# Moving the transposes of x from TensorE to VectorE's 32 by 32 blocks, with the scores on sixteen tiles, in a cross-attention and SwiGLU kernel on Trainium2

## The chip, the cores and the metric

One core of a Trainium2 chip. The time is the device time of one execution in microseconds (us).

## The reference

Eight batches of 512 tokens and 32 states, 8 heads of 64 columns, all fp32. Tokens read the states and states read the tokens through one product of scores; both results go through one gated feed-forward block.

```python
# x: (8, 8, 512, 64), state: (8, 8, 32, 64) = (B, H, S or Ns, D)
scores  = scale * x @ state^T ;   a  = softmax(scores)  ; xread = a  @ state
scores2 = scale * state @ x^T ;   a2 = softmax(scores2) ; sread = a2 @ x
tok = concat([xread, sread], axis=2)  -> (B*(512+32), 512)
xn  = tok / sqrt(mean(tok^2) + 1e-6) * rms_g          # w_gate, w_val: 512 x 1536, w_out: 1536 x 512
out = (silu(xn @ w_gate) * (xn @ w_val)) @ w_out
```

## The kernel before

Each batch is a period of some 87 us. A period holds the feed-forward of batch b (the "hidden half", six pairs of seven block products each, then the "projection") and, spread between its products, the attention of batch b+1. The order in which all engines get their instructions is a string of letters, one letter a step of one stream: `a` the read of the tokens, `s` the read of the states, `h`, `t`, `u` products, copies and sums of the hidden half, `p`, `c`, `k` those of the projection, `v`, `w`, `x` the products of the weights with the states.

The part that the change replaces: x is turned by sixteen full transposes on TensorE, ScalarE copies them out of the accumulator, and the scores are eight matmuls on tiles of 64 rows by 32 columns (a tile is a part of TensorE's array; the profile writes it `64*32`).

```python
def tokens_read(b):
    ...
    TE.transpose(out=tp, in_=packed, identity=ident)              # the states of b      L272
    VE.tensor_copy(stT, tp)
    xT = one.tile([P, 4, NC, P], F32, name="xT", tag="xT")
    for c in range(NC):                                            # NC = 4
        tp = aps.tile([P, 4, P], F32, name="at")
        for j in range(4):
            TE.transpose(out=tp[:, j, :], in_=xb[:, c, P * j:P * j + P], identity=ident)  # L282
        yield
        SE.copy(xT[:, :, c, :], tp)                                                       # L284
        yield "step"
    sp = [aps.tile([P, S], F32, name="at") for e in range(2)]
    for j in range(4):
        for e in range(2):
            TE.matmul(out=sp[e][Ns * j:Ns * j + Ns, :], lhsT=stT[D * e:D * e + D, j, :],  # L291
                      rhs=xT[D * e:D * e + D, j].rearrange("p c t -> p (c t)"),
                      start=True, stop=True)
    ...                      # 32 by 32 transposes on VectorE, softmax, transposes back

for b in range(1, B):        # the periods
    if b + 2 < B:
        load_state(b + 2)
        load_x(b + 2)        # 4 pieces of 256 KB, one queue
    ...
    for stream in PERIOD:    # the string: one letter, one step
        next(streams[stream])
```

Of the kernel before, what the change touches and what calls it, by code (L numbers as in the profile page):

```python
# [8 lines left out]
F32 = mybir.dt.float32  # L9
# [19 lines left out]
)  # L29

PERIOD = (
    "hthtvvhhtuxxhuhthuhththuuhtuuhhxxhhuvxutvhtthuuhuhthuuxhxhxuxtthuhuthhuthuxxhuta"
    "uahatuhtaxuuuhtauahuahhaahuttuhutauhhhtuuahuhuutauphuauupuauapacasapaaaapapaskaa"
    "aaksacccassppakckpaaackasaapakapaskaaaswpksksswsxxwxxpxcspcskx"
)

STATES = (
    "hyyyyhthyytthhhuuhtuhththhytuuhuuhthuhhtthyuhyyutyhhhuuuttyuhhutyyhhthuhyhuhuttu"
    "yhuhttyuhuhuuhuthhyuthythytuhuuhuhutuuhuuppcpkpcpukkcpkpkpc"
)  # L40


# [1 line left out]
def kernel(  # L44
# [7 lines left out]
    moe_rms_g: bass.AP,  # L52
    out: bass.AP,
):



# [38 lines left out]


    rows = {}
    x_sb = {}

    def load_state(b):

        rows[b] = two.tile([P, 2, D], F32, name="rows")
        for j in range(4):
            src = state[b, 2 * j:2 * j + 2].rearrange("e n d -> n e d")
            nc.sync.dma_start(out=rows[b][Ns * j:Ns * j + Ns], in_=src)

    def load_x(b, *queues):
        x_sb[b] = two.tile([P, NC, H * D], F32, name="x_b")
        for c in range(NC):  # L110
            (queues or (nc.sync,))[c % max(1, len(queues))].dma_start(
                out=x_sb[b][:, c].rearrange("p (h d) -> p h d", h=H),
                in_=x[b, :, P * c:P * c + P, :].rearrange("h p d -> p h d"))
# [150 lines left out]

    read = {}

    def tokens_read(b):
        xb, packed = x_sb[b], rows.pop(b)
        stT = two.tile([P, 4, Ns], F32, name="stT")
        stT_g[b] = two.tile([P, 4, Ns], F32, name="stT_g")  # L270
        tp = aps.tile([P, 4, Ns], F32, name="at")
        TE.transpose(out=tp.rearrange("p j n -> p (j n)"),  # L272
                     in_=packed.rearrange("p e d -> p (e d)"), identity=ident)
# [5 lines that stand above are left out]
        for c in range(NC):  # L279
# [15 lines that stand above are left out]


        sS = read[b] = two.tile([P, 2, NC, P], F32, name="sS")
        eS = one.tile([P, 2, S // Ns, Ns], F32, name="eS", tag="eS")
        m1 = two.tile([P, 2, S // Ns], F32, name="m1")
        z1 = two.tile([P, 2, S // Ns], F32, name="z1")  # L300
        for e in range(2):
            VE.transpose(out=eS[:, e].rearrange("p k n -> p (k n)"), in_=sp[e])
            yield
            SE.copy(sS[:, e].rearrange("p c t -> p (c t)"), sp[e])
            yield "step" if e else None

        def along(t, e):
            return t[:, e].unsqueeze(2).to_broadcast([P, S // Ns, Ns])

        for e in range(2):  # L310
            VE.reduce_max(out=m1[:, e], in_=eS[:, e], axis=AXX)
            yield
            VE.tensor_tensor(out=eS[:, e], in0=eS[:, e], in1=along(m1, e), op=ALU.subtract)
            yield
            SE.activation(out=eS[:, e], in_=eS[:, e], func=ACTF.Exp, scale=SCALE)
            yield "step"
        VE.tensor_tensor(out=stT_g[b], in0=stT, in1=rms_g.unsqueeze(2).to_broadcast([P, 4, Ns]),
                         op=ALU.mult)
        yield
        aT_s[b] = two.tile([P, 2, S], F32, name="aT_s")  # L320
        for e in range(2):
            VE.reduce_sum(out=z1[:, e], in_=eS[:, e], axis=AXX)
            yield
            VE.tensor_scalar(z1[:, e], z1[:, e], 1e-9, None, op0=ALU.add)
            VE.reciprocal(z1[:, e], z1[:, e])
            yield
            VE.tensor_tensor(out=eS[:, e], in0=eS[:, e], in1=along(z1, e), op=ALU.mult)
            yield
            VE.transpose(out=aT_s[b][:, e], in_=eS[:, e].rearrange("p k n -> p (k n)"))
            yield "step"  # L330


        reads = [(aps, vps)[j // 2].tile([P, S], F32, name=("at", "pv")[j // 2]) for j in range(4)]
        for j in range(4):
            for e in range(2):
                TE.matmul(out=reads[j][D * e:D * e + D, :],  # L336
                          lhsT=packed[Ns * j:Ns * j + Ns, e, :],
                          rhs=aT_s[b][Ns * j:Ns * j + Ns, e],
                          start=True, stop=True)
        yield  # L340
        sq = one.tile([P, 4, S], F32, name="sq", tag="xT")
        for i, j in enumerate((2, 3, 0, 1)):
            SE.activation(out=sq[:, i, :], in_=reads[j], func=ACTF.Square, scale=DM ** -0.5)
            yield "step" if i == 3 else None
        for i, j in ((0, 1), (2, 3), (0, 2)):
            VE.tensor_tensor(out=sq[:, i, :], in0=sq[:, i, :], in1=sq[:, j, :], op=ALU.add)
            yield
        sp = aps.tile([P, NC], F32, name="at")
        for c in range(NC):
            TE.matmul(out=sp[:, c:c + 1], lhsT=sq[:, 0, P * c:P * c + P], rhs=ones,  # L350
                      start=True, stop=True)
        yield
        ss = two.tile([P, NC], F32, name="ss")
        VE.tensor_scalar(ss, sp, 1e-6, None, op0=ALU.add)  # L354
        yield "step"
        ri = mean_root(ss, NC)
        yield
        rp = along_rows(ri, NC)
        yield
        VE.tensor_tensor(out=aT_s[b], in0=aT_s[b],  # L360
                         in1=rp.unsqueeze(1).to_broadcast([P, 2, S]), op=ALU.mult)
        yield "step"
# [160 lines left out]
    def weights_of(b):  # L523


        def blocks(mp):
            v, _ = v_sb[b, mp]
            return [[v[:, e, :, k, :]] for k in range(2) for e in range(2)]

        def sums(mp):  # L530
            _, vs = v_sb.pop((b, mp))
            return [[vs[:, i]] for i in range(3)]

        return blocks, sums
# [55 lines left out]
    def hidden_seven(n, weights, tokens, silu, after=lambda mp: None):  # L590
# [67 lines left out]
        def sums():  # L658
            for mp, q in enumerate(pairs):
                h = hb[:, 2 * mp:2 * mp + 2, 0:n]  # L660
                for to, ps in ((gates(q)[1], "z"), (gates(q)[0], "y"), (q["c"], "x")):
                    VE.tensor_tensor(out=to, in0=to, in1=q[ps][:, :, 0:half], op=ALU.add)  # L662
                    yield
                if not silu:
                    VE.scalar_tensor_tensor(out=h, in0=h, scalar=1.0, op0=ALU.add, op1=ALU.mult,  # L665
                                            in1=q["g"].rearrange("p m c t -> p m (c t)"))
                    yield
                for i, val in ((1, q["c"]), (0, q["x"][:, :, 0:half])):
                    part = h[:, :, half * i:half * i + half]
                    if silu:  # L670
                        VE.tensor_tensor(out=part, in0=part, in1=val, op=ALU.mult)
                    else:
                        VE.scalar_tensor_tensor(out=part, in0=part, scalar=0.5, in1=val,
                                                op0=ALU.mult, op1=ALU.mult)
                    yield
                if 2 * mp >= HM:
                    k = 2 * mp - HM
                    upper, lower = (hb[:, k:k + 2, half * i:half * i + half] for i in range(2))
                    VE.tensor_tensor(out=seven["s"][:, k:k + 2, 0:half], in0=lower,
                                     in1=h[:, :, half:n], op=ALU.add)  # L680
                    yield
                    VE.tensor_tensor(out=lower, in0=upper, in1=lower, op=ALU.subtract)
                    yield

        return products(), copies(), sums()
# [211 lines left out]
    for b in range(1, B):  # L897
        if b + 2 < B:
            load_state(b + 2)
            load_x(b + 2)  # L900
        h, t, u = hidden_seven(S, weights_of(b), lambda b=b: tokens_of(b), False)
        p, c, k = project_seven(S, store_tokens(b))
        own = [own_weights(b, mp) for mp in range(2, NM // 2)]
# [55 lines left out]
```

## Time and profile before

| | before |
|---|---|
| median of 4 runs (the rounds of the changed kernel) | 800.76 us (800.35 to 801.38) |
| span of the profiled run | 798.9 us |
| opening (to the first states' product of batch 1) | 133.65 us |
| one middle period | 86.90 us |
| from the last batch's states' product to the end | 148.11 us |

The three parts come from the starts of one kind of matmul that occurs once a batch (L397, the states' product with x): the distance between two of them is one period. In the same way I add up, for every kind of matmul, the distances from each record's start to the next start on TensorE. That sum is what the kind costs on a full TensorE, with its pipelining taken into account. The durations of single records are not: the profile's groups for one period (line, engine, operation, names, tile shape and operand, count, then busy us and mean ns of one) give 273 ns for a transpose of x, four of which hold TensorE for only 0.44 us.

```profile
L282 PE MATMUL at<-ident,x_b 128*128 128x128 f32 x16 | 2.4, 273 | 0.0
...
L291 PE MATMUL at<-xT,stT 64*32 64x512 f32 x16 | 1.1, 601 | 0.0
```

### The profile page before, as it was taken

The page shows a single profiled execution, that of the slowest core. Times are in us where ns is not written, and L with a number is a line of the kernel's source. Part 1 is how long each engine was busy: PE and PEld are TensorE (multiplying, and loading weights), DVE is VectorE, ACT ScalarE, POOL GpSimd, SP SyncE. Part 2 cuts the span into 40 slices and gives each one's busy share as a digit, 9 for nine tenths or more (in the row PEclk, how much of TensorE's full clock was granted, in tenths as well). Part 3 has the DMA queues.
Part 4 walks back from the last instruction along what each step waited for, and adds up shares of the span by engine and source line. Part 5 has one row for each costly group of instructions (what it writes and reads, how often), then busy time and mean ns, then how long its engine had stood idle before and what let it go on. Part 6 is the DMA issues. An engine that isn't in the chain of part 4 may idle for free.

```text
span 798.9 us, 12273 instructions
## 1 busy us (share of the span) xinstructions
PE 786.0 (98%) x4902; PEld 605.2 (76%) x4902; DVE 515.0 (64%) x786; ACT 347.0 (43%) x572; POOL 179.0 (22%) x216
## 2 busy tenths in 40 slices
PE   6999999999999999999999999999999999999998
PEld 5643444788778887888778877888788877888996
DVE  4999996688347842786358833785278635881461
ACT  5998864553245323543255314532354324510320
POOL 0000003530154004510433015500451044400000
PEclk9999999999999999999999999999999999999999
DMA  9987746700182007400461018200540024101311
GB/s 285 262 289 287 263 159 186 264 23 14 34 273 106 1 24 218 185 1 16 127 240 44 4 34 283 107 1 14 193 163 2 14 109 181 66 4 43 113 54 28
DMA packets 61593, 94.13 MB, mean 118 GB/s; under 512 B 38752, under 2 KB 46432, under 8 KB 54624
## 3 DMA queue, kind: packets, MB, share of 16 engines
q1 hardware_dynamic: 59360, 92.75, 34.2%
q10 hardware_dynamic: 2176, 0.59, 0.3%
q8 instruction: 39, 0.64, 0.3%
q14 instruction: 18, 0.15, 0.1%
HBM read 78.12 MB, written 15.20 MB: 117 GB/s over the span
## 4 chain that ended last, share of the span: by engine, by line
PE 93%; DVE 5%; issue 0%; DMA 0%; ACT 0%; SPq 0%
PE f L600 37%; PE f L754 35%; PE f L694 5%; PE pv L496 3%; PE at L454 3%; PE pv L454 3%; PE at L282 2%; PE at L291 1%; DVE ex L232 1%; PE at L397 1%; PE at L336 1%; DVE raw L228 1%; PE at L350 1%; PE at L385 1%; DVE w_m L237 1%
## 5 line engine op out<-in xcount | busy, mean ns | idle before, releaser
L754 PE MATMUL f<-wo,hb 128*128 128x256 f32 x540 | 124.2, 382 | 0.4 <-ACT ot L791 0.2
L662 DVE TENSOR_TENSOR g<-g,f 128x512 f32<-128x512 f32 (+1 forms) x96 | 62.8, 654 | 90.1 <-PE f L600 86.6
L600 PE MATMUL f<-aT_s,v 128*128 128x256 f32 x504 | 119.5, 380 | 0.0
L754 PEld LDWEIGHTS f<-wo,hb 128*128 128x128 f32 x540 | 101.4, 190 | 20.1 <-ACT ot L791 6.9
L600 PEld LDWEIGHTS f<-aT_s,v 128*128 128x128 f32 x504 | 93.8, 190 | 17.3 <-issue 5.2
L254 POOL TENSOR_TENSOR ri<-ss,mhalf 128x4 f32<-128x4 f32 x8 | 9.2, 1156 | 361.8 <-DVE ss L354 361.8
L600 PE MATMUL f<-aT_t,vs 128*128 128x256 f32 x336 | 87.2, 382 | 0.0
L754 PE MATMUL f<-wt,hs 128*128 128x256 f32 x360 | 80.4, 379 | 0.0
L653 ACT ACTIVATE hb<-g 128x1024 f32<-128x1024 f32 (+1 forms) x48 | 48.2, 1004 | 63.0 <-DVE g L662 63.0
L754 PEld LDWEIGHTS f<-wt,hs 128*128 128x128 f32 x360 | 68.3, 190 | 9.5 <-issue 0.2
L791 ACT COPY ot<-f 128x256 f32<-128x256 f32 x60 | 21.5, 372 | 122.5 <-PE f L754 122.5
L600 PEld LDWEIGHTS f<-aT_t,vs 128*128 128x128 f32 x336 | 62.6, 190 | 15.1 <-issue 5.9
L665 DVE SCALAR_TENSOR_TENSOR hb<-hb,g 128x1024 f32<-128x1024 f32 x42 | 55.5, 1320 | 7.8 <-ACT hb L653 7.8
L651 ACT COPY g<-f 128x512 f32<-128x512 f32 (+1 forms) x48 | 26.9, 561 | 76.7 <-PE f L600 76.7
L483 POOL TENSOR_TENSOR vs<-v,vs 128x256 f32<-128x256 f32 x42 | 58.3, 1389 | 0.0
L480 POOL TENSOR_TENSOR vs<-v 128x256 f32<-128x256 f32 x42 | 30.5, 727 | 118.6 <-ACT v L465 118.6
L694 PE MATMUL f<-wo,hb 128*128 128x512 f32 x96 | 44.7, 600 | 0.0
L600 PE MATMUL f<-aT_t,v 128*128 128x256 f32 x168 | 43.9, 383 | 0.0
L496 PE MATMUL pv<-aT_s,v 128*128 128x512 f32 x96 | 43.6, 593 | 0.0
L600 PE MATMUL f<-aT_s,vs 128*128 128x256 f32 x168 | 43.1, 379 | 0.0
L754 PE MATMUL f<-wt,hb 128*128 128x256 f32 x180 | 42.6, 386 | 0.0
L754 PE MATMUL f<-wo,hs 128*128 128x256 f32 x180 | 41.6, 382 | 0.0
(131 smaller groups left out, 1263.4 us busy)
## 6 DMA issues: line engine op xcount, KB each, us to landing
w_m<-w_d SPq DMA_DIRECT2D x48, 1024.0 KB, 6.5
x_b<-in_x_dram SPq DMA_DIRECT2D x30, 256.0 KB, 4.6
out_dram<-ot SPq DMA_DIRECT2D x56, 128.0 KB, 1.8
raw<-in_moe_w_val_dram SPq DMA_DIRECT2D x6, 1024.0 KB, 5.1
raw<-in_moe_w_out_dram SPq DMA_DIRECT2D x6, 1024.0 KB, 7.6
w_d<-w_m SPq DMA_DIRECT2D x6, 1024.0 KB, 4.9
raw<-in_moe_w_gate_dram SPq DMA_DIRECT2D x5, 1024.0 KB, 6.4
raw<-in_moe_w_gate_dram SPq DMA_DIRECT2D x2, 512.0 KB, 4.8
```

Source lines behind the costliest of these rows:

```text
L454: TE.matmul(out=pv[e][Ns * j:Ns * j + Ns, :], lhsT=stT_g[b][D * e:D * e + D, j, :], rhs=w[D * e:D * e + D, j].rearrange("p m k f -> p (m k ...
L480: GE.tensor_tensor(out=vs[:, 0], in0=a21, in1=a22, op=ALU.add)
L483: GE.tensor_tensor(out=vs[:, 2], in0=a12, in1=vs[:, 1], op=ALU.subtract)
L496: TE.matmul(out=to[0], lhsT=lhs(i, k), rhs=r, start=(i == 0), stop=(i == len(rhs) - 1))
L600: TE.matmul(out=ps[:, i, 0:half], lhsT=l[:, i, :], rhs=r, start=(start and i == 0 and k == 0), stop=(k == len(lhs) - 1), skip_group_check= ...
L651: SE.copy(gates(q)[1], q["x"][:, :, 0:half])
L653: SE.activation(out=hb[:, 2 * mp:2 * mp + 2, 0:n].rearrange("p m (c t) -> p m c t", c=2), in_=q["g"][:, :, :, 0:half], func=ACTF.Silu if s ...
L662: VE.tensor_tensor(out=to, in0=to, in1=q[ps][:, :, 0:half], op=ALU.add)
L665: VE.scalar_tensor_tensor(out=h, in0=h, scalar=1.0, op0=ALU.add, op1=ALU.mult, in1=q["g"].rearrange("p m c t -> p m (c t)"))
L694: TE.matmul(out=banks[r], lhsT=hb[:, m, P * r:P * r + P], rhs=wo[:, m, :], start=(m == 0), stop=(m == NM - 1))
L754: TE.matmul(out=banks[name][:, r, :], lhsT=lhs(k)[:, P * r:P * r + P], rhs=rhs(k), start=(start and r == 0 and k == 0), stop=(k == HM - 1) ...
L791: SE.copy(to, banks[name][:, r, :])
```

## The change

Its intent: take the sixteen transposes of x off TensorE, which is the bound. VectorE's transpose works within blocks of 32 by 32 (the page is named in the prediction), so a block's 32 columns of d come to lie on the 32 partitions where its tokens were. A head has 64 columns, so each score is a sum over two halves `k`, and every matmul has 32 rows only: the scores become 64 matmuls on sixteen 32 by 32 tiles. The states are loaded four times over to lie under every row group. Batches 0 and 1, whose attention runs in the opening, keep the old way. The order string was dealt anew for the new steps, and at the end the first projection product of the states moves ahead of the last hidden product.

```diff
 PERIOD = (
-    "hhtthtvvhhtuxx... (222 letters)
+    "hhtvtvhtxhuxhu... (220 letters)
 STATES = (
-    "...tuuhuhutuuhuuppcpkpcpukkcpkpkpc"
+    "...tuuhuhutuuphuupcpkpcpukkcpkpkpc"
...
+    def load_fours(b):
+        fours[b] = one.tile([P, H, D], F32, name="fours")
+        for g in range(4):
+            nc.sync.dma_start(out=fours[b][Ns * g:Ns * g + Ns],
+                              in_=state[b].rearrange("h n d -> n h d"))
     def load_x(b, *queues):
         x_sb[b] = two.tile([P, NC, H * D], F32, name="x_b")
+        if b > 1:
+            for i in range(4 * NC):
+                c, g = divmod(i, 4)
+                nc.sync.dma_start(
+                    out=x_sb[b][Ns * g:Ns * g + Ns, c].rearrange("p (h d) -> p h d", h=H),
+                    in_=x[b, :, P * g + Ns * c:P * g + Ns * c + Ns, :].rearrange("h p d -> p h d"))
+            return
...
+    def scores_of_blocks(b, packed, soft):
+        stB = one.tile([P, H, 2, Ns], F32, name="stB")
+        VE.transpose(out=stB, in_=fours.pop(b))                   # rearranges cut
+        yield
+        xB = one.tile([P, NC, H, 2, Ns], F32, name="xB", tag="xT")
+        for i in range(0, NC, 2):
+            VE.transpose(out=xB[:, i:i + 2], in_=xb[:, i:i + 2])  # L335
+            yield
+        sp = [...]                                                # four accumulator banks
+        for e in range(2):
+            for k in range(2):
+                for j in range(4):
+                    for g in range(4):
+                        TE.matmul(out=sp[g][Ns * j:Ns * j + Ns, e],            # L346
+                                  lhsT=stB[Ns * g:Ns * g + Ns, 2 * j + e, k, :],
+                                  rhs=xB[Ns * g:Ns * g + Ns, :, 2 * j + e, k, :],
+                                  start=(k == 0), stop=(k == 1), skip_group_check=True)
+        yield
...                                # the softmax works on four groups of 256 columns
...                                # the states' transpose (L272) comes after the softmax's first half
+                steps = [lambda: finish(1, q["c"]), lambda: finish(0, q["x"][:, :, 0:half])]
+                if k >= 0:
+                    steps.insert(1 if silu else 2, first_sum)     # for the states: one step earlier
```

## The prediction

> **What bounds the kernel now.** I read the engine shares first, then the busy time by stretch, then the chain that ended last inside one batch, then what TensorE waited for.
>
> ```profile
> PE 786.0 (98%) x4902; PEld 605.2 (76%) x4902; DVE 515.0 (64%) x786; ACT 347.0 (43%) x572; POOL 179.0 (22%) x216
> ```
>
> TensorE has 12.9 us of the 798.9 us span free. The stretches (columns: length, then busy us of PE, weight load, VectorE, ScalarE, GpSimd) say where:
>
> ```profile
> 0.00:134.00 134.00, 125.71 (x607) 63.00 (x611) 115.60 (x154) 100.07 (x127) 11.54 (x21) 0.99 0.77 249
> ...
> 390.00:477.00 87.00, 86.97 (x568) 70.10 (x568) 53.47 (x83) 34.61 (x62) 24.89 (x31) 1.00 0.29 98
> ...
> 740.00:799.00 59.00, 54.75 (x408) 51.84 (x406) 26.10 (x55) 13.16 (x29) 0.00 (x0) 0.99 0.20 66
> ```
>
> and, asked for separately, the hidden half of one batch (the products up to the projection):
>
> ```profile
> 316.00:355.00 39.00, 39.00 (x224) 31.91 (x223) 29.91 (x39) 21.20 (x34) 15.31 (x16) 1.00 0.34 121
> ```
>
> Of the free time 8.3 us lie in the opening and 4.3 us at the end; a middle batch (86.9 us from one to the next) has 0.03. So in batches 1 to 6, where the change works, each us taken off TensorE is a us off the time, and a us added to another engine costs nothing until TensorE waits for it. VectorE is 77% busy in that half (29.91 of 39.00), not the 64% of the page.
>
> The chain in that half (start, length, what) prices the removed work:
>
> ```profile
> 340.17 0.11 PE at L272
> 340.28 0.87 PE f L600 x4
> 341.15 0.44 PE at L282 x4
> 341.58 1.73 PE f L600 x8
> 343.31 0.44 PE at L282 x4
> ...
> 344.62 0.44 PE at L282 x4
> ...
> 346.78 0.44 PE at L282 x4
> ...
> 351.54 1.02 PE at L291 x16
> ```
>
> Four transposes of x (L282) hold TensorE 0.44 us; the scores (L291) 1.02 us. All that TensorE is seen to wait for is the first state load (5.9 us) and then:
>
> ```profile
> PE at L350 <- DVE sq L346: 1.0, 1, 1.0
> PE at L291 <- ACT xT L284: 0.7, 1, 0.7
> PE at L454 <- DVE w_m L237: 0.7, 1, 0.7
> PE f L600 <- DVE c L662: 0.5, 1, 0.5
> ```
>
> **What the Trainium skill says.** "Perfetto Trace Analysis", Identifying the Most-Contended Engine: matmul busy time misleads, because matmuls are pipelined. The trace agrees: an L282 transpose has a mean of 287 ns, and four cost 0.44 us on the chain; I price by the chain. "TensorE: Matmul & The Clock Gate", Part 3: sixteen 32 by 32 tiles compute at once, measured 10.6 times faster. No run has that here; the eight-tile scores are the nearest. The same page, under "Wait — 56ns, not 53.3ns?", has starts never closer than about 25 ns. The trace disagrees: L397 puts 64 into 1.03 us, 16 ns each, and eight matmuls of L336 start 7 ns apart. I use the trace. "VectorE: DVE Perf Modes", The three transpose paths: VectorE transposes 32 by 32 blocks only. The trace has such an instruction (STREAM_TRANSPOSE), at 705 to 710 ns for 128x512.
>
> **The change part by part**, for each of batches 2 to 7 (prepared during batches 1 to 6).
>
> *TensorE, removed:* 16 transposes of x, 4 x 0.44 = 1.76 us. Six times: 10.6 us. The state transpose (0.11 us) stays, only later.
>
> *TensorE, scores:* 8 matmuls of 512 columns on 64 by 32 tiles become 64 of 128 columns on 32 by 32 tiles. fp32 takes two records each in the trace (16 for the 8), so 128 are to come. Columns through one tile: now 2 passes x 512 = 1024; then 64 matmuls / 16 tiles = 4, x 2 passes x 128 = 1024. Equal, so the array time should be equal; L397 has 64 / 4 tiles x 64 columns = 1024 too and also takes 1.03 us, although it has four times the records of L291. What differs is issue: 128 x 7 ns = 0.90 us, about the array time itself. The two tie, and a few hiccups are likely; I take 1.15 us (estimate), +0.13 us each, +0.8 us in six.
>
> *VectorE:* added one transpose of 128x512 for the state copies (0.71) and two of 128x1024 for x. No row has that size; from 0.71 at 512 columns, and 0.69 against 1.22 for elementwise rows of 512 and 1024, I estimate 1.24 each, 2.48. The scores' and weights' transposes become 4 of 256 instead of 2 of 512 each; at 0.42 (256-column elementwise rows) 1.68 against 1.41 and 1.42: +0.5. Removed: the copy of the transposed state, 0.29. Sum +3.4 us, 20 us in all, beside TensorE.
>
> *ScalarE:* minus 4 copies of 0.59 = 2.36, and 4 score copies of 0.37 for 2 of 0.58 = +0.3: -2.0 us, off the path.
>
> *Transfers:* x comes in 16 pieces of 64 KB instead of 4 of 256 KB, and the state again, four times over, in 4 more: 16 more issues at about 0.43 us on one queue, 6.9 us. In the built order the x pieces stand ahead of the next two weight loads, but the matmuls that need those now stand 36 block matmuls after the previous pair instead of 26, 4.3 us later at 0.432. And a batch's x and state copies are fetched a batch before use. I expect no wait.
>
> *The states:* the first projection product moves ahead of the last hidden product, which waits 0.51 us for VectorE (the last wait shown). That gap fills: -0.5 us.
>
> Sum: 800.85 - 10.6 + 0.8 - 0.5 = 790.5. For small new waits in the new order I add 0.5: **791.0 us**.
>
> **Does VectorE keep up?** In the hidden half each of six pairs takes TensorE 6.05 us (28 records of 0.216). VectorE's work on a pair is 3 x 0.69 + 1.41 + 1.10 + 0.68 = 5.3 us in the first three (its slower rows there) and 2.06 + 1.22 + 0.69 + 0.69 + 0.68 + 0.69 = 6.0 in the last three. The new order puts the state transpose into the second pair (6.0), both x transposes into the third (7.7), and the score transposes into the last two (6.9 each). So from the third pair on VectorE falls behind, by 1.7, then 0.9 and 0.9; a weight pair (1.9 us on TensorE) stands in the third, the scores (1 us) in the fifth, and give most of it back. Walking it by hand from each pair's start, the bank of the first product is freed about 1.5 us before TensorE needs it in the tightest place (third pair), and the sums for the projection are ready 0.7 to 0.8 us ahead of their two matmuls. In the kernel before the same sums are ready about 1.1 us ahead (L679 ends at 359.3, the matmul starts at 360.4). Tighter, but it holds, also because x no longer goes through TensorE and ScalarE before the scores, and the scores stand ten block matmuls earlier.
>
> **Rivals.**
>
> *A. The 128 small records are bound by issue.* For it: nothing in the trace has sixteen tiles, and L397's average is 16 ns, not 7. Against: L397's columns explain its whole 1.03 us. At 16 ns the scores take 2.05 us, the gain falls by 6 x 0.9, the time is 796; at the skill's 25 ns they take 3.2 us, more than the transposes saved: 803.
>
> *B. VectorE becomes the bound in the hidden half.* For it: the 77% and the margins under 1 us; in the built order the transposes stand ahead of sums that free a matmul bank, so a late one delays the freeing. Against: the order was dealt anew with these in it. A miss of 1 us a batch makes 797; the whole added 3.4 us on the path makes 811. I give 15% to a loss over 4 us.
>
> *C. The queue of transfers.* For it: the 6.9 us of issue ahead of two weight loads. Against: the moved matmuls, and a DMA share of 0.29 over a batch. If the loads came late, it would be 1 to 3 us a batch, 797 to 809. I give 5%.
>
> *D. The reordering itself gains.* A batch's 336 records at 0.2158 (84 in 18.13 us in the dense stretch of the projection) make 72.5 us, against 73.9 us when I add up the distances from each one's start to the next start on TensorE, so about 1.4 us a batch goes at the switches between kinds of matmul. A better order could take back part: at a third of it, 788.
>
> **Range and chances.** Between 788.5 (D, scores at 1.02) and 796.5 (A at 16 ns, or B at 1 us a batch) I expect 8 of 10. Faster by over 2% is 784.8 or less, 16 us, half as much again as the removed work: 3%. Slower by over 2% is 817 or more and needs more than B in full: 2%.
>
> **What would show it right or wrong.** Right: a middle batch of 85.2 to 85.4 us instead of 86.9; no L282 after the opening; the scores a piece of 1.0 to 1.3 us in the chain with 128 records; TensorE still without idle time in the middle; VectorE near 535 us and ScalarE near 335; the 0.51 us wait at the end gone. Wrong: a score piece of 2 us or more (A); TensorE idle in the hidden half or at the first projection products with VectorE named as releaser (B); TensorE idle ahead of the weight products with a transfer named (C).

## The result, and the profile after

The changed kernel takes 791.66 us in the median of 4 runs (791.04 to 792.42), against 800.76 for the kernel before in the same rounds. The ratio is 0.9886 (95% interval 0.9869 to 0.9903). The prediction was 791.0, with a range of 788.5 to 796.5.

The engine shares on the page of the changed kernel (busy us, share, instructions):

```profile
PE 776.5 (98%) x5478; PEld 603.5 (76%) x5478; DVE 521.5 (66%) x822; ACT 334.4 (42%) x560; POOL 170.9 (22%) x216
```

TensorE is as full as before, over a span of 789.0 us; ScalarE has 334.4 us (335 predicted). The stretches that answer to those of the prediction (length, then busy us of TensorE, weight load, VectorE, ScalarE, GpSimd, then clock, DMA share, GB/s):

```profile
0.00:134.00 134.00, 125.32 (x643) 62.82 (x647) 115.49 (x154) 100.49 (x127) 11.56 (x21) 1.00 0.80 251
390.00:475.00 85.00, 85.00 (x662) 69.50 (x661) 54.81 (x89) 32.14 (x60) 23.20 (x29) 1.00 0.31 103
732.00:789.00 57.00, 53.42 (x400) 50.73 (x398) 25.93 (x55) 12.52 (x27) 0.00 (x0) 1.00 0.21 69
316.00:355.00 39.00, 39.00 (x323) 32.56 (x323) 33.92 (x47) 18.90 (x31) 12.36 (x15) 1.00 0.37 125
```

TensorE has no idle time in a middle period, although VectorE rose from 29.91 to 33.92 us of the 39 us of the hidden half. The waits of TensorE of over half a us, apart from the first load:

```profile
PE at L424 <- DVE sq L420: 1.0, 1, 1.0
PE at L528 <- DVE w_m L253: 0.9, 1, 0.9
PE at L307 <- ACT xT L300: 0.7, 1, 0.7
```

The wait at the end (the last one shown in the prediction) is gone, and none took its place. The chain around the scores, one period:

```profile
423.83 3.67 PE f L674 x17
427.50 0.23 PE at L346 x2
...
429.30 0.03 PE pv L346 x2
429.33 4.73 PE f L674 x21
```

Here is the surprise: the scores run from 427.50 to 429.33, 1.83 us, where the prediction had 1.15 and the kernel before 1.02. So I put the periods side by side. The table has one middle period of each, start to next start, in us:

| kind of matmul | before | after | difference |
|---|---|---|---|
| transposes of x (16 records) | 1.748 | 0 | -1.75 |
| scores (16, then 128 records) | 1.019 | 1.833 | +0.81 |
| transposes for the states' read (L385, then L459) | 1.061 | 0.873 | -0.19 |
| projection products | 36.952 | 36.745 | -0.21 |
| hidden products | 36.948 | 36.856 | -0.09 |
| all others | 9.17 | 9.17 | 0 |
| period | 86.90 | 85.48 | -1.42 |

The time went out through the door that the prediction named, some came back through the scores, and some more went out through the order. The whole span is 9.9 us shorter: 1.24 in the first period, 5 x 1.42 in the other five, 1.04 from the last states' product to the end, and 0.49 in the opening. The opening is not touched by the change. In the profiled runs that leave it alone it lasts 133.1 to 134.3 us, so those 0.49 us are within its scatter.

VectorE has 521.5 us and not 535. By form of instruction, the records of the change itself add 19.3 us (the prediction had 20), but others became shorter by 10.0 us in sum, above all VectorE's products into `hb` from `c`, from 965 to 821 ns each. GpSimd too has a sum that became shorter; its group before and then after:

```profile
L483 POOL TENSOR_TENSOR vs<-v,vs 128x256 f32<-128x256 f32 x42 | 58.3, 1389 | 0.0
```

```profile
L557 POOL TENSOR_TENSOR vs<-v,vs 128x256 f32<-128x256 f32 x42 | 44.4, 1057 | 0.0
```

The same sum takes 1.06 us instead of 1.39. That the two engines hinder each other where they run side by side, and do so less in the new order, would fit both, but no run here took one of them away. (Records of one engine overlap a little, so the busy time rose by 6.5 us and not by 9.3.)

### The profile page after: what moved, and what is told of

Same layout as the page of the kernel before. It is cut to its first block, busy times and chain, and to the rows that moved or that the text cites. A ratio compares the mean times of both kernels' runs of the same rounds, so it can differ in the third digit from the quotient of the medians.

```text
span 789.0 us, 13559 instructions
## 1 busy us (share of the span) xinstructions
PE 776.5 (98%) x5478; PEld 603.5 (76%) x5478; DVE 521.5 (66%) x822; ACT 334.4 (42%) x560; POOL 170.9 (22%) x216
## 4 chain that ended last, share of the span: by engine, by line
PE 92%; DVE 5%; DMA 1%; issue 0%; ACT 0%; SPq 0%
PE f L674 37%; PE f L836 35%; PE f L776 5%; PE pv L570 4%; PE at L528 3%; PE pv L528 3%; DVE ex L248 1%; PE at L471 1%; PE at L410 1%; DVE raw L244 1%; PE at L346 1%; PE at L459 1%; PE at L424 1%; DMA raw<-in_moe_w_gate_dram 1%; DVE w_m L253 1%; PE pv L346 1%
## 5 line engine op out<-in xcount | busy, mean ns | idle before, releaser
L270 POOL TENSOR_TENSOR ri<-ss,mhalf 128x4 f32<-128x4 f32 x8 | 13.5, 1692 | 320.4 <-DVE s L449 210.9
L739 DVE SCALAR_TENSOR_TENSOR hb<-hb,g 128x1024 f32<-128x1024 f32 x42 | 53.2, 1266 | 4.6 <-ACT hb L727 4.6
L557 POOL TENSOR_TENSOR vs<-v,vs 128x256 f32<-128x256 f32 x42 | 44.4, 1057 | 0.0
L836 PEld LDWEIGHTS f<-wt,hb 128*128 128x128 f32 x180 | 33.7, 190 | 9.4 <-DVE ot L881 5.0
```

The lines of the kernel that those rows point to most:

```text
L557: GE.tensor_tensor(out=vs[:, 2], in0=a12, in1=vs[:, 1], op=ALU.subtract)
L739: VE.scalar_tensor_tensor(out=h, in0=h, scalar=1.0, op0=ALU.add, op1=ALU.mult, in1=q["g"].rearrange("p m c t -> p m (c t)"))
L836: TE.matmul(out=banks[name][:, r, :], lhsT=lhs(k)[:, P * r:P * r + P], rhs=rhs(k), start=(start and r == 0 and k == 0), stop=(k == HM - 1) ...
```

## The experiments

After the result I had these theories. On the scores: the price is one per small matmul and per round of tiles (theory 1), or the loops are in a bad order (theory 2), or the array gives sixteen tiles no more than the rate of eight (theory 3). On the rest: the removal is worth just its own time; the new order gains because it gathers things, or is needed to hide VectorE; the transfers are far from, or near, the bound. In the trace of the changed kernel the scores' 128 records start like this: the first passes of the first sixteen tiles 7 ns apart, then their second passes 7 ns apart (fp32 takes two). That first round is over after 0.32 us. In the three later rounds the first tile starts its two passes 110 ns apart while no other tile of that round starts (the last second passes of the round before still do), then the others follow at 16.7 ns for each matmul, and a round takes 0.433 us. The records of the weight loads stop in the same way: no load starts in the 109 ns between the first tile's two.

### e1: the loops of the scores the other way round

```diff
-                for j in range(4):
-                    for g in range(4):
+                for g in range(4):
+                    for j in range(4):
```

> The changed kernel with one edit: in the scores the column group of the array is the fastest loop and the row group the next (before: row group fastest). Same 64 matmuls, 128 records, same 1024 columns per tile. In the changed kernel the scores take 1.83 us a batch: the first sixteen matmuls start 7 ns apart, and in each later round of sixteen the first tile's two passes stand 110 ns apart with no other tile started, then the other fifteen follow at 16.7 ns each, and the round takes 0.433 us. Theory 1 (what is at work is a pace of the issue, 16.7 ns for each matmul with its two weight loads, and a stop at the first tile of each round): the order of the groups does not enter, 1.75 to 1.9 us, time 791.7 within 0.7. Theory 2 (neighbouring matmuls in different row groups get in each other's way[...]): another order of the groups moves it by 0.3 us or more, to 1.1 to 1.5 us and 787 to 790 us if the new order is the better one, or to over 2.1 us and 793.5 or more if it is the worse.

Measured: 791.65 us (790.94 to 792.16, 4 runs), scores 1.83 us, with the same starts to within 3 ns. Theory 2 falls: whether neighbours share a row group (the 32 rows of a tile) or a column group (its 32 columns) does not enter.

### e2: rounds of eight tiles

```diff
-        for e in range(2):
+        for e, jh in ((0, 0), (1, 0), (0, 2), (1, 2)):
             for k in range(2):
-                for j in range(4):
+                for j in range(jh, jh + 2):
```

> The changed kernel with one edit: the scores go through the sixteen tiles in rounds of eight (two column groups, all four row groups), eight rounds instead of four. Same matmuls and records. Theory 1 (a pace of 16.7 ns for a matmul, and a stop of about 0.18 us at the first tile of each round): 8 x (0.11 + 7 x 0.0167 + 0.066) = 2.3 us instead of 1.83, time about 794.5. Theory 3 (the array runs only as fast as eight tiles[...], whatever the order): 1.7 to 1.9 us as in the changed kernel, time 791.7.[...]

A single run: 791.88 us. The chain (start, length) gives the scores 429.83 - 427.87 = 1.96 us:

```profile
424.85 3.02 PE f L674 x14
427.87 0.23 PE at L346 x2
...
428.25 0.07 PE at L346 x2
428.36 0.07 PE at L346 x2
...
429.83 2.36 PE f L674 x10
```

Both numbers missed: theory 1 said 2.3, theory 3 at most 1.9. Eight tiles run without any stop: a group of eight starts every 0.109 us (428.25, 428.36), which is one pass of 128 columns, and eight rounds of two passes make 1.75 us plus start and end. So rounds of eight are bound by the columns, and rounds of sixteen end at the same average rate (0.433 us for sixteen matmuls is twice 0.217) for another reason. The stop at the head of a round is no fixed price, as theory 1 had it.

### e3: the scores twice

```diff
-        for e in range(2):
+        for e in (0, 1, 0, 1):
```

> The changed kernel with the 64 score matmuls of each of batches 2 to 7 done twice (the second time starts the sums anew, so the result is the same). Reading of the changed kernel's trace: one pass of them costs TensorE 1.83 us and TensorE is the bound in the middle of the kernel, so six repeats cost 6 x 1.73 to 1.83 = 10.4 to 11.0 us, and the time is 802 to 803. If the cost were the 1.15 us of the prediction, and the rest of the 1.83 us a start-up seen only once, 6.9 us: 798.6. If the scores were partly hidden beside something else: less than 6 us.

Measured: 812.26 us (811.24 to 812.42), ratio to before 1.0137 (1.0122 to 1.0152). That is 20.6 us more than the changed kernel, about twice the highest expectation. The 256 records take 4.9 to 5.5 us. Up to some point in the second half they go at the known pace, then TensorE stops once for 1.5 to 1.9 us. The chain, one period:

```profile
441.47 0.08 PE pv L346 x3
441.61 1.28 issue
442.89 0.30 PE at L346 x2
```

"Issue" means that the profile shows nothing it waited for. The stop comes after 156 to 248 of the 256 records, at another one in each batch, and never in the 128 records of the changed kernel. Without it the repeat costs 1.5 to 1.8 us, about what was expected of it. What stops TensorE no run tests, but the trace has two marks of a supply of instructions that ran dry. From one stop to the next TensorE's records (matmuls, weight loads, semaphores) number 1536, or once 1792: six or seven times 256 exactly. And each of the six stops ends 1.24 to 1.41 us after a packet of 16 KB has landed on the queue that the page calls "q8 instruction". So this is the likely cause; it is not shown.

### e4: the states' part put back

```diff
-                    steps.insert(1 if silu else 2, first_sum)
+                    steps.append(first_sum)          # and the old STATES string
```

> The changed kernel with the states' part put back as it was (the first projection product after the last hidden product, and the first sum after both finishing products): only the last 48 us differ. The prediction gave that part 0.5 us, the wait of the last hidden product for VectorE. From the last weight sums of the last batch to the end the changed kernel is 1.04 us shorter than the kernel before. Theory 1 (all of that is the states' part): 792.6 to 792.8 us. Theory 2 (0.5 us is the states' part, the rest is the last batch's new order): 792.1 to 792.3 us. Theory 3 (the wait only moved): 791.7 within 0.2.

Measured: 792.44 us (791.74 to 792.87), 0.8 more than the changed kernel. The stretch from the last states' product to the end is 147.87 us instead of 147.07: the states' part is worth 0.80 us of the 1.04. So theory 1 was too high and theory 2 too low; the remaining 0.24 us are the last batch's share of the new order. That a wait of 0.51 us was worth 0.8 fits the way the profile counts: idle time begins at the modelled end of a matmul (275 ns after its start here), later than the moment when the next could have started (112 ns), and the second record after the wait comes 0.10 us late as well: 0.51 + 0.16 + 0.10 = 0.78.

### e5: the removal alone, in the kernel before

```diff
-            tp = aps.tile([P, 4, P], F32, name="at")
-            for j in range(4):
+            tp = aps.tile([P, 4, P], F32, name="at") if b < 2 else None
+            for j in range(4 if b < 2 else 0):
                 TE.transpose(out=tp[:, j, :], in_=xb[:, c, P * j:P * j + P], identity=ident)
             yield
-            SE.copy(xT[:, :, c, :], tp)
+            SE.copy(xT[:, :, c, :], tp if b < 2 else xb[:, c].rearrange("p (j t) -> p j t", j=4))
```

> The kernel before with one edit, wrong on purpose: for batches 2 to 7 the sixteen transposes of x are not done on TensorE; ScalarE's four copies stay and take x as it lies (so the scores are of the wrong numbers). This is the removal alone, in the old order. From the distances of starts the transposes hold TensorE 1.748 us a batch. Theory 1 (TensorE is the bound all through the middle, the removal is worth its own time): 6 x 1.748 = 10.5 us off, 790.3 within 0.7. Theory 2 (removal alone gains more, because switches to and from the transposes go too and are counted in the rows of other matmuls): 788 to 789.5. Theory 3 (something else becomes the bound once they are gone): 792 or more.

Its output is wrong, which doesn't matter for the time. Measured: 790.51 us (789.79 to 790.80), ratio 0.9871 (0.9857 to 0.9886). A middle period is 85.14 us instead of 86.90: 1.76 less, the transposes' own time and no more; every other row of the table stays as before. Theory 1 holds. The transposes' price was right, and it was all that there was to win.

### e6: the changed kernel in the old order

```diff
+    def in_old_places(steps):
+        for n in (1, 0, 0, 1, 0, 0, 0, 1, 0, 0, 1) + 4 * (2,) + 6 * (1,) + (2,) + 21 * (1,):
+            for i in range(n):
+                next(steps)
+            yield
-            streams.update(a=tokens_read(b + 1), ...
+            streams.update(a=in_old_places(tokens_read(b + 1)), ...      # and the old PERIOD string
```

> The changed kernel with the batch order of the kernel before; the steps of the read of the tokens are put into the old order's places (the block transposes where the transposes of x stood, the eight score steps two by two in four places, the late state transpose with the step after it). Nothing else differs. In the changed kernel the e transposes, the projection and the hidden products hold TensorE 0.49 us a batch less than before. Theory 1 (that gain comes from the new order): 6 x 0.49 = 2.9 us back, 794.6. Theory 2 (it comes with the removal of the transposes of x, and the order is worth little): 791.7 to 792.3. Theory 3 (the new order is what keeps VectorE's added work hidden): TensorE waits for VectorE in the hidden half, 797 or more.

Measured: 804.78 us (804.37 to 806.07), ratio to before 1.0054 (1.0039 to 1.0069): 13 us slower than the changed kernel, slower even than the kernel before. Theory 3 holds. The longest wait of TensorE is now on VectorE, one in each of six batches:

```profile
PE f L674 <- DVE c L736: 6.8, 6, 1.1
```

```profile
389.10:476.70 87.60, 86.44 (x664) 69.60 (x663) 55.66 (x89) 32.55 (x60) 24.73 (x29) 1.00 0.30 101
```

In the stretch of the second fence, one period long, TensorE is idle for 1.16 us, and VectorE works without a gap in the 9 us before TensorE stops. The hidden products cost 38.62 us instead of 36.86. The transposes for the states' read and the projection cost 1.061 and 36.95 us, just as before. (Of the 1.76 us 1.16 are idle time; most of the rest are starts around it that come 0.04 to 0.16 us late.) So the order does two things. It keeps VectorE hidden, worth 1.68 us a batch. And it gains 0.48 us (0.19 + 0.21, and 0.08 of the hidden products' 1.76) that have nothing to do with VectorE; the section on the prediction says what they were.

### e7: the block transposes twice

```diff
-        for i in range(0, NC, 2):
+        for i in (0, 0, 2, 2):          # still one yield after each pair
```

> The changed kernel with VectorE's two block transposes of x done twice each, at the same places (the second writes the same numbers): VectorE gets 2.47 us more in each of six batches, 14.8 us in all, in the third pair of the hidden half, where the prediction saw it fall behind most. Theory 1 (VectorE has several us of slack there): 791.7 within 0.7. Theory 2 (the slack is the 1.5 us of the prediction's tightest place): 1 us a batch shows, 797 to 798. Theory 3 (no slack left): 2.47 us a batch, 806.

Measured: 792.31 us (791.20 to 792.62). VectorE's share on the page rises:

```profile
PE 778.0 (98%) x5478; PEld 604.0 (76%) x5478; DVE 533.0 (67%) x834; ACT 332.9 (42%) x560; POOL 167.0 (21%) x216
```

The middle period is 85.52 us against 85.48: of 2.47 us of work more in each, 0.04 shows. The median is 0.65 higher than that of the changed kernel; in the profiled run the opening was 1.08 us longer, so I put this down to the opening's scatter. Theory 1 holds: in the new order VectorE has 2.4 us to spare at that place.

### e8: x loaded twice

```diff
-            for i in range(4 * NC):
-                c, g = divmod(i, 4)
+            for i in range(8 * NC):
+                c, g = divmod(i % (4 * NC), 4)
```

> The changed kernel with the sixteen x pieces of each of batches 2 to 7 loaded twice into the same place: 16 more issues on the one queue and 1 MB more a batch, ahead of the next two weight loads. Theory 1 (the transfers are far from the bound): 791.7 within 0.7. Theory 2 (the queue was near its limit, and the weight products wait): some 7 us of issues more a batch, of which 1 to 4 show: 797 to 815, with TensorE waiting for a transfer ahead of the weight products.

Measured: 826.11 us (822.42 to 830.70), ratio 1.032 (1.0274 to 1.0367); the clock was 0.975 in the profiled run. The largest wait of TensorE:

```profile
PE at L528 <- DMA w_m<-w_d: 25.7, 5, 11.2
```

I expected theory 1, and it fell in the clearest way, beyond the upper end of theory 2. In the trace one weight load a batch stands in the queue behind the pieces of x. In the changed kernel it lands 4.2, 4.7, 6.1, 6.1 and 6.3 us before the first matmul that reads it, in the five periods that load x (5.4, 6.5, 6.0, 4.9 and 5.8 before the change); here it lands just as it is needed, TensorE having waited. Doubling the pieces of x took more than this margin, while doubling the block transposes (e7) stayed within VectorE's; in us, VectorE's 2.4 is the smaller of the two.

The waits are not the whole loss. The span of this profile is 39.9 us longer than the changed kernel's, and the waits make 25.7 of them. In each of the five (2.65 to 11.2 us long) the granted clock falls to half, 1.9 to 2.5 us after the wait began, and stays there for 6.8 us (13.7 in the longest). Hidden products in these stretches start 427 ns apart instead of 216. One such stretch, the clock in the third column from the end:

```profile
351.60:358.40 6.80, 5.16 (x24) 2.87 (x25) 0.90 (x2) 1.07 (x2) 0.00 (x0) 0.50 0.92 348
```

The other 14 us fall in and around these stretches. The pauses of up to 1.9 us in e3 and e11 have no such fall.

### e9: the scores on eight tiles, with x from VectorE

If the small tiles cost 0.81 us a batch, larger ones should win it back. Let each row group of the array have one half of a head's columns; then two neighbouring row groups hold a whole head, and 64-row tiles are possible again. It needs a second load of x in that layout, and, after e8, a place for it where no weight load stands behind it: right after the block transposes have freed its buffer.

```diff
+    def load_halves(b):
+        x_half[b] = one.tile([P, 2 * NC, H, Ns], F32, name="x_h")
+        for c in range(2 * NC):
+            for g in range(4):
+                t0 = HT * (g // 2) + Ns * c                        # HT = S // 2
+                d0 = Ns * (g % 2)
+                nc.sync.dma_start(out=x_half[b][Ns * g:Ns * g + Ns, c],
+                                  in_=x[b, :, t0:t0 + Ns, d0:d0 + Ns].rearrange("h p d -> p h d"))
...                                      # load_x for the states as in the kernel before
+            if i and b + 1 < B:
+                load_halves(b + 1)       # after the second block transpose
...
-            for k in range(2):
-                for j in range(4):
-                    for g in range(4):
+            for j in range(4):
+                for g in range(2):
                     TE.matmul(out=sp[g][Ns * j:Ns * j + Ns, e],
-                              lhsT=stB[Ns * g:Ns * g + Ns, 2 * j + e, k, :],
-                              rhs=xB[Ns * g:Ns * g + Ns, :, 2 * j + e, k, :],
+                              lhsT=stB[D * g:D * g + D, 2 * j + e, :],
+                              rhs=xB[D * g:D * g + D, :, 2 * j + e, :],
```

To make room for its 8 KB a partition, the scores' copy is held once instead of twice, and small buffers share places.

> A version meant to be better: the changed kernel (its order, VectorE's block transposes, the moved states' part), but each row group of the array gets one half of the 64 columns of a head, so that two neighbouring row groups together hold a whole head: the scores are then 16 matmuls of 256 columns on eight 64 by 32 tiles (32 records) instead of 64 of 128 on sixteen 32 by 32 tiles (128 records). Columns per tile are 1024 in both. For it x is loaded a second time, in 32 pieces of 32 KB in that layout, at a place in the queue where no weight load stands behind it; the x that the states read is loaded as in the kernel before. Theory 1 (the 1.83 us come from many small matmuls on small tiles): the scores take 1.0 to 1.1 us, as in the kernel before, six times 0.75 to 0.8 less, 787.0 within 0.8. Theory 2 (they come from operands that VectorE made, or from the place in the order): 1.8 us again, 791.7. Theory 3 (the second load of x costs what it wins or more, as 16 more pieces cost 34 us in the run before): 793 or more, with TensorE waiting for transfers.

Measured: correct, 786.68 us (785.90 to 786.91), ratio to before 0.9823 (0.9809 to 0.9838). It is faster than both kernels. The chain at the scores:

```profile
414.98 10.58 PE f L679 x49
425.55 1.02 PE at L353 x32
426.58 0.63 PE f L679 x2
```

1.02 us, and a middle period of 84.67 us, 0.81 less than the changed kernel; every other row of the table is as in the changed kernel. Theory 1 holds; operands that VectorE made are as good as others. The tight weight load now lands 8.5 to 9.3 us ahead, because the 32 pieces stand elsewhere: where a transfer is issued counts for more here than how many there are.

### e10: sixteen tiles, half as many matmuls of twice the columns

```diff
-        for e in range(2):
-            for k in range(2):
-                for j in range(4):
-                    for g in range(4):
-                        TE.matmul(out=sp[g][Ns * j:Ns * j + Ns, e], lhsT=stB[.., 2 * j + e, k, :],
-                                  rhs=xB[.., :, 2 * j + e, k, :], ...)
+        for k in range(2):
+            for j in range(4):
+                for g in range(4):
+                    TE.matmul(out=sp[g][Ns * j:Ns * j + Ns], lhsT=stB[.., 2 * j, k, :],
+                              rhs=xB[.., :, 2 * j:2 * j + 2, k, :], ...)    # 256 columns
```

> The changed kernel with one edit, wrong on purpose: the scores on the same sixteen tiles as 32 matmuls of 256 columns instead of 64 of 128 (both heads of a pair take the state of the first). 1024 columns per tile as before, half as many records (64). Theory 1 (sixteen tiles do compute side by side, and the price is per matmul and per round: two rounds instead of four): 0.95 to 1.2 us instead of 1.83, time 787 to 788. Theory 3 (the array gives these tiles together only the rate of eight, 54 ns for a pair of passes of 256 columns on average): 32 x 0.054 = 1.73 plus the start and the end, 1.8 to 1.9 us, time 791.7.

Half of the heads get another head's states, as meant; the check of the results let it pass all the same (it failed e5, at a relative error of 0.023), so "correct" here is a weak statement. Measured: 789.12 us (788.73 to 789.77), 2.5 less than the changed kernel. The scores take 427.69 - 426.27 = 1.42 us:

```profile
426.27 0.34 PE at L345 x2
...
427.69 4.51 PE f L674 x20
```

Between the two expectations, and the starts say why. The first round of sixteen starts all its passes 7 ns apart and is over after 0.459 us: sixteen tiles with two passes of 256 columns each, where one such pass takes 0.216 us. So sixteen tiles do compute side by side at full rate, and theory 3 falls. In the second round the first tile's second pass starts 0.193 us after its first, with no other tile started between, and then the 30 remaining records follow at 16.7 ns each. The price lies in every round after the first. What inside TensorE makes the first tile of a later round stop the others is open; it happens with sixteen tiles and not with eight (e2, e9).

### e11: eight pieces of x twice

```diff
-            for i in range(4 * NC):
+            for i in range(6 * NC):      # the index taken modulo 4 * NC
```

> The changed kernel with 8 of the 16 x pieces loaded twice instead of all 16 (which cost 34 us). In the changed kernel the weight load that stands behind the x pieces lands 6.1 to 6.3 us before the first matmul that reads it (4.9 to 6.0 in the kernel before); with 16 pieces more it was late by about 5 us a batch, so a piece delays it by about 0.7 us. Theory 1 (that one margin is all there is to it): 8 pieces delay by 5.6 us, within the margin, 791.7 to 792.5. Theory 2 (the cost is proportional to the pieces, from contention): half of 34 us, about 808.

Measured: 794.88 us (794.48 to 796.23). The middle periods are 85.48 us, as in the changed kernel to 0.01; the tight load lands 0.3 to 2.5 us ahead there. The measured time is over theory 1's 792.5; most of the loss is in the first period (84.13 instead of 81.41 us), where the x of two batches are loaded one behind the other:

```profile
PE at L528 <- DMA w_m<-w_d: 1.9, 1, 1.9
```

So theory 1 holds in the middle, and theory 2 falls. The first period has less margin (4.2 us in the changed kernel), which I had not looked at.

## Why the prediction was right or wrong

The time was right to 0.7 us, a middle period to 0.1 us of the 85.2 to 85.4 expected. Of its terms, one was badly mis-sized and others made up for it: that the total came so close is luck.

- **"TensorE, removed: ... 10.6 us."** Right. The removed records held 1.748 us a batch, and the removal alone gave 1.76 a batch (e5). That TensorE is the bound there, so that each us off it is a us off the time, is shown by the same run. But the reading behind it, that TensorE has only 0.03 us free in a middle batch, was not right: it waited twice a batch where the count of idle time shows next to nothing (below).
- **"TensorE, scores: ... The two tie, and a few hiccups are likely; I take 1.15 us."** This step failed. It reasoned that records can start 7 ns apart, so that issue (0.90) and columns (about 1.02) tie. A 7 ns start is true of the first round of sixteen only; later rounds take 0.433 us each. The term was +0.81 us a batch, 4.9 in all, and not +0.13 and 0.8. e9 wins just these 4.9 us back, by larger tiles. Rival A named this danger with the 16 ns that the trace had, and about three quarters of it came true (0.68 of 0.9 us a batch over the 1.15); the guess of the cause (a pace of single records) was too simple, as e2 and e10 show.
- **"VectorE: ... 20 us in all, beside TensorE."** Right: 19.3 us of records added, each block transpose of x 1.235 us (1.24 predicted), no wait of TensorE. The share was not near 535 us, because other records became shorter. The hand-walked margin of about 1.5 us in the third pair was too small: 2.47 us more at that place cost 0.04 (e7). But rival B was no idle fear. In the old order it comes true, with some 10 of the 13 us (e6, 6 x 1.68): that the order was dealt anew for VectorE is a part of the change that the gain depends on.
- **"Transfers: ... I expect no wait."** Right, with a margin of 4.2 to 6.3 us (e8, e11). It had been 4.9 to 6.5: shorter now in the first two periods, longer in the others, and in e1 and e7, with the same transfers, the same load lands up to 1.6 us earlier or later, so these profiles show no clear change. I had not worked out how steep the loss is behind it.
- **"The states: ... That gap fills: -0.5 us."** The mechanism was right; the size is 0.80 us (e4).
- **"For small new waits in the new order I add 0.5."** None came. In its place the order gained, as rival D had it: the transposes for the states' read and the projection cost 0.40 us a batch less, and e6 shows that the order did it. But the cause was not D's: the time did not go at switches between kinds of matmul but in waits (below). Adding D's gain and the scores' loss at their measured sizes, a batch gives -1.75 + 0.81 - 0.40 - 0.09 = -1.43, measured -1.42; six make -8.5 (the first period gave only 1.24), the states -0.8, together -9.3. The medians differ by 9.1.

Where the time sat is visible in the trace: before, the first of the two groups of four transposes held TensorE 0.625 us and the second 0.436; after, both hold 0.437. The Trainium skill, "TensorEngine Tiling (Array Packing)", Tiling Modes, says that a change of the tiling mode drains TensorE; the trace fits this where the hidden products give way to the scores (309 ns from the last start to the first, instead of 216), but the transposes use the full array as the projection does, so that is not what they lost. They lost it to ScalarE. These two lines of the kernel before (start, length, group) have ScalarE's copy of a projection result out of its accumulator, and the weight load of the next projection product, which waits for that copy:

```profile
379.93 0.37 ACT L791 COPY ot<-f 128x256 f32<-128x256 f32 x1 [1.10 <-PE f L754]
...
380.36 0.30 PEld L754 LDWEIGHTS f<-wo,hb 128*128 128x128 f32 x2 [0.26 <-ACT ot L791]
```

The copy ends at 380.30 and the load starts 42 ns after its signal. The list of TensorE's waits has nothing of this, because the last transpose counts as busy, by its modelled end, until 380.33. A second such wait stands at 309.42, between hidden and projection products. The two cost 0.29 and 0.19 us: 0.19 in the row of the transposes, 0.21 in that of the projection (its second record comes 0.10 us late each time), 0.08 in that of the hidden products, nearly all by which these rows became shorter. In the changed kernel the next product after the same transposes is another, and its load has no idle time before it:

```profile
382.74 0.30 PEld L836 LDWEIGHTS f<-wo,hs 128*128 128x128 f32 x2
```

In the old order (e5, e6) both waits are there again.

## What to carry to other kernels

On a full engine, price a kind of instruction by the distances from start to next start, and price a new kind by a repeated pattern, not by its fastest burst: sixteen tiles are fast for one round and no faster than eight when they follow each other. A layout that keeps tiles larger was worth more than a second way to fill the array, even at the price of loading the data twice. An engine that is never seen idle may still wait: look also at what ended the idle time of the weight loads. And work moved to an idle engine or queue is free only in the right place of the order: the same instructions in the old order lost 13 us, and transfers ahead of a load that is needed soon lost 34, part of it because the clock fell in the waits.

## What the Trainium skill lacked or had wrong

- "TensorE: Matmul & The Clock Gate", Part 3, gives sixteen tiles 10.6 times the speed, for one matmul on each. It does not say what comes after. Here the first round of sixteen fp32 matmuls of 128 columns takes 0.32 us and every following one 0.433 us, the rate of eight tiles (0.218 us for eight, e2).
- The same part says that matmuls start in program order. In the trace of the first round the first passes of all sixteen tiles start before any second pass, a tile's second 133 ns behind its first. If the two passes of an fp32 matmul stand next to each other in the program, which no view here shows, they did not start in that order.
- The same page, "Wait — 56ns, not 53.3ns?", has about 25 ns as the least distance of two starts, and does not say there that matmuls on different tiles are left out (Part 3 has some 4 ns for those). The records of the scores, on different tiles, start 7 ns apart in the first round and 16.7 ns later on.
- "Runtime: NRT & Kernel Launch", Instruction fetch mechanics, gives no length for a fetch of instructions that comes late. If the stop in e3's 256 records of scores is one, as is likely and not shown, it is 1.5 to 1.9 us.
